# Attention beside a small expert: the output matrix M built by head groups, its rows placed by DMA, and two spread products on GpSimd

## The chip, the cores and the metric

One NeuronCore of one Trainium2 chip. The metric is device time in microseconds of one execution; lower is better. Engines are called PE (TensorE), DVE (VectorE), ACT (ScalarE), POOL (GpSimd) and SP (SyncE, which only issues DMAs here). PSUM has eight banks of 512 float32 columns, numbered 0 to 7.

## The reference

x has 2048 rows (tokens) of D = 640 columns in bfloat16. It is normalized, and three terms are added:

```python
xn = _layernorm(x)                                  # per row
# A: linear attention, H = 32 heads of Dh = 20 columns
qkv = (xn @ wqkv); q, k, v = ...                    # each 2048 x 640
phi = lambda t: jnp.where(t > 0, t + 1, jnp.exp(t)) + 1e-6
pq, pk = phi(q), phi(k)
kv = einsum("bhsd,bhse->bhde", pk, v)               # 20 x 20 for each head
z  = einsum("bhsd->bhd", pk)
o  = (pq @ kv) / (pq . z + 1e-6)                    # for each head and token
A  = o @ wo
# B: the 8 tokens with the largest xn @ w_r go through a gated MLP of F = 1536
y  = (silu(x_sel @ w_gate) * (x_sel @ w_up)) @ w_down * sigmoid(r_sel)
B  = xn + scatter of y to the 8 rows
out = x + A + B
```

## The kernel before

The order of the work on each engine is the order in which the program is written: nothing is scheduled by a planner. Tokens come in T = 16 tiles of 128.

First stage (to about 57 us in the profile): each tile is normalized, transposed into `xnT`, multiplied by the k weights (L249), turned into `pk` by exp and relu on ACT and a minimum and add on DVE (`k_phi`, L271), and summed into G = xn^T pk (`g1`, L278). Blocks of q, 128 columns by 512 tokens, are put in between: `q_mm(u)` (L286) on PE, `q_act` (L295, L296) on ACT, and `q_phi` (L302) on DVE, which writes `pqT`. Blocks 0 to 7 are made here, 8 to 19 later; block u belongs to tokens (u // 5) x 512 and rows (u % 5) x 128 of `pqT`. `eq` and `rq` have three buffers each. POOL makes x + xn in place of x (`add_s`, L219); SP stores it to `s_dram` (L110), because the expert's rows are added there by a scatter, and later loads it back into `x_sb` (L769).

Denominators: `den(h)` (L584) makes 1 / (pq . z) for half h of the tokens, as rows by heads. They have to be spread from 32 heads to 640 rows of `pqT`. For half 0 this goes through DRAM: ACT stores `rden` repeated 20 times to `rd` (L623), SP loads it as `spr`, in two DMAs (`rden_in`, L629), and DVE multiplies `pqT` by it for 256 tokens at a time (`rden_mul(j)`, L636, j = 0 to 3; tokens j x 256, that is output tiles 2j and 2j + 1). For half 1 it goes through PE (`spread_mm`, L596), ACT (`spread_copy`, L610) and DVE (`spread_mul`, L617), between output tiles.

The middle stage: kv = G^T wv for six heads at a time (`kv_mm`, L642; 120 columns, the sixth group 40), masked to the head blocks by `kv_out` (L650) and written to `kvz`. Then M = blockdiag(kv) wo, 640 x 640, which needs 128-row blocks for the output product. A group has 120 rows, so `kvz` is laid out with zeros between the groups (offset 248), and `m_unit(m)` makes the 128 rows of block m from the two groups that touch it: two groups by two halves of 320 columns, four products (L661) and one copy to `Ms` (L666). `kvz` is zeroed by a memset on DVE at the start (L136). The expert runs here too: gate and up products (L720), the down product (L749), and its four column pieces times the gate, taken from one PSUM bank by ACT and DVE in turn (L761, L763) into `y8`; POOL scatters `y8` onto `s_dram` (L764). The order on PE from there is q12, the down product, q13, unit 0, q14, unit 1, q15, unit 2, q16, unit 3, q17, unit 4, q18, q19, with q blocks in banks 2 and 3 in turn.

The output stage: for each tile t, `o_mm(t)` (L799) multiplies `pqT` by `Ms` in ten products of 320 columns, `o_out(t)` (L808) adds `x_sb` on DVE and starts the store, on SP for even t and ACT for odd t (L813). Banks alternate, so tile t + 2 waits for `o_out(t)`. After tile 0 PE does `den(1)`, which reads the q blocks 10 to 19. The last tile (`o_last`) goes out in three pieces: 320 and 160 columns by SP, and 160 by ACT (L837).

DMAs issued from SP and ACT use eight semaphores in turn; a DMA waits until the one that used its semaphore before has landed. DMAs of one issuing engine are issued in program order.

Of the kernel before, what the change touches and what calls it, by code (L numbers as in the profile page):

```python
# [8 lines left out]
P = 128  # L9
S = 2048  # L10
D = 640
# [3 lines left out]
T = S // P  # L15
KC = D // P
FC = F // P
C = 8
HW = 320
HG = 120  # L20
NG = 6
WS = 248
KVW = 1664
FJ = F // 4
QW = D // 4
EPS_BF16 = 1.0013580322265625e-05
# [2 lines left out]
BF16 = mybir.dt.bfloat16  # L29
# [4 lines left out]
ALU = mybir.AluOpType  # L34
# [3 lines left out]
def kernel(  # L38
# [12 lines left out]
    nc = tc.nc  # L51
    V, A, G, PE = nc.vector, nc.scalar, nc.gpsimd, nc.tensor
# [15 lines left out]
    ps = psum.tile([P, 8, 512], F32, tag="ps", name="ps")  # L68
    rd = tc.dram_tile([4, D, 256], BF16, name="rd")
# [9 lines left out]
    wv = big.tile([P, KC, D], BF16, tag="wv", name="wv")  # L79
    wo = big.tile([P, NG, D], BF16, tag="wo", name="wo")  # L80
    wg = big.tile([P, KC, F], BF16, tag="wg", name="wg")
    wu = big.tile([P, KC, F], BF16, tag="wu", name="wu")
    wd = big.tile([P, FC, D], BF16, tag="wd", name="wd")
    kvz = big.tile([P, KVW], BF16, tag="kvz", name="kvz")

    SP = nc.sync
# [32 lines left out]
    def load_cols(w, lo, hi, base):  # L119
        SP.dma_start(w[:, lo:hi, :], wqkv_v[:, lo:hi, base : base + D])  # L120

    w_jobs = {
        6: [lambda: kcw(wg, B_w_gate, 0, 3)], 8: [lambda: kcw(wg, B_w_gate, 3, 5)],
        10: [lambda: kcw(wu, B_w_up, 0, 3)], 12: [lambda: kcw(wu, B_w_up, 3, 5)],
        13: [lambda: load_cols(wv, 0, 3, 2 * D), lambda: load_cols(wv, 3, 5, 2 * D), load_wo],
    }

    def load_wd(lo, hi):
        SP.dma_start(wd[:, lo:hi, :], B_w_down.rearrange("(fc p) n -> p fc n", p=P)[:, lo:hi, :])

    w_jobs[14] = [lambda: load_wd(0, 6), lambda: load_wd(6, FC)]

    zw = sb("zw", [P, 512])
    V.memset(zw[:], 0.0)
    xsT = sb("xsT", [P, KC, H])
    V.memset(kvz[:], 0.0)  # L136
    V.memset(xsT[:], 0.0)
    mhalf = sb("mhalf", [P, 2])
    G.memset(mhalf[:], -0.5)
# [143 lines left out]
    def q_mm(u, bank=7):  # L283
        tb, m = u // KC, u % KC
        for kc in range(KC):
            PE.matmul(  # L286
                ps[:, bank, :], lhsT=wq[:, kc, m * P : (m + 1) * P],
                rhs=xnT[:, kc, tb * 512 : (tb + 1) * 512],
                start=(kc == 0), stop=(kc == KC - 1),
            )  # L290

    def q_act(u, bank=7):
        e = evq.tile([P, 512], BF16, tag="eq", name=f"eq{u}")
        r = evq.tile([P, 512], BF16, tag="rq", name=f"rq{u}")
        A.activation(e[:], ps[:, bank, :], AF.Exp)  # L295
        A.activation(r[:], ps[:, bank, :], AF.Relu)  # L296
        kev["q", u] = e, r

    def q_phi(u):
        tb, m = u // KC, u % KC  # L300
        e, r = kev.pop(("q", u))
        V.scalar_tensor_tensor(  # L302
            out=pqT[:, m, tb * 512 : (tb + 1) * 512], in0=e[:], scalar=1.0, in1=r[:],
            op0=ALU.min, op1=ALU.add,
        )

    def q_ev(u, bank=7):
        q_act(u, bank)
        q_phi(u)
# [315 lines left out]
            rden[:, 0, :].unsqueeze(1).to_broadcast([P, DH, 256]),  # L625
        )

    def rden_in(j):
        SP.dma_start(  # L629
            spr[:, j * KC : (j + 2) * KC, :],  # L630
            rd[j : j + 2, :, :].rearrange("j (m p) t -> p (j m) t", p=P),
        )

    def rden_mul(j):
        sl = pqT[:, :, j * 256 : (j + 1) * 256]
        V.tensor_tensor(out=sl, in0=sl, in1=spr[:, j * KC : (j + 1) * KC, :], op=ALU.mult)  # L636

    def kv_mm(gs, bank):
        for i, g in enumerate(gs):
# [6 lines left out]
                )  # L646

    def kv_out(g0, n, w, bank, o):
        a = P + WS * g0
        V.tensor_tensor(  # L650
            out=kvz[0:w, a : a + WS * n].rearrange("p (g f) -> p g f", g=n)[:, :, 0:w],
            in0=ps[0:w, bank, o : o + n * w].rearrange("p (g f) -> p g f", g=n),
            in1=mask[0:w, 0:w].unsqueeze(1).to_broadcast([w, n, w]), op=ALU.mult,
        )

    def m_unit(m, b0, eng):
        for i, g in enumerate((m, m + 1)):
            w = HG if g < 5 else 40
            a = g * 256 + (P if i == 0 else 0)
            for b in range(2):  # L660
                PE.matmul(  # L661
                    ps[:, b0 + b, 0:HW], lhsT=kvz[0:w, a : a + P],
                    rhs=wo[0:w, g, b * HW : (b + 1) * HW], start=(i == 0), stop=(i == 1),
                )
        dst = Ms[:, m, :].rearrange("p (b f) -> p b f", b=2)
        eng(dst, ps[:, b0 : b0 + 2, 0:HW])  # L666


    for t in range(T):
# [37 lines left out]
    spare = big.tile([P, T, D], BF16, tag="xn", name="spare")  # L707
    spr = spare[:, 0:8, :].rearrange("p a b -> p (a b)").rearrange("p (r f) -> p r f", f=256)
    Ms = late[:, 0:KC, :]
    for j in (0, 2):  # L710
        rden_in(j)
    A.copy(GT[:, 0:4, 512:D], ps[:, 2, :].rearrange("p (c f) -> p c f", c=4))
    A.copy(GT[:, 4, 512:D], ps[:, 3, 0:P])
    kv_mm(range(0, 4), 4)
# [2 lines left out]
    for a, w in enumerate((wg, wu)):  # L717
        for kc in range(KC):
            for j in range(4):
                PE.matmul(  # L720
                    ps[32 * j : 32 * j + 32, a, 0:FJ].rearrange("p (b f) -> p b f", f=32), lhsT=xsT[:, kc, :],
                    rhs=w[:, kc, :].rearrange("p (b j f) -> p j b f", j=4, f=32)[:, j],
                    start=(kc == 0), stop=(kc == KC - 1), tile_position=(0, 32 * j),
                )
    eg = late[:, 9:13, :].bitcast(F32).rearrange("p a b -> p (a b)")[:, 0 : 2 * FJ]
    eg = eg.rearrange("p (a b) -> p a b", a=2)
    ub = late[:, 5, 0:FJ]
# [14 lines left out]
    V.tensor_mul(hm, gu, eg[:, 1, :])  # L742
    hT = late[:, 8, 0:FJ]
    V.transpose(hT, hm)
    q_ev(11, 2)
    q_mm(12, 3)
    for fc in range(FC):
        for i in range(4):
            PE.matmul(  # L749
                ps[32 * i : 32 * i + 32, 1, 0:QW], lhsT=hT[:, 32 * fc : 32 * fc + 32],  # L750
                rhs=wd[:, fc, i * QW : (i + 1) * QW],
                start=(fc == 0), stop=(fc == FC - 1), tile_position=(0, 32 * i),
            )
    q_ev(12, 3)
    q_mm(13, 2)
    y8 = sb("y8", [C, D])
    for i in range(4):
        y_o, y_i = y8[:, i * QW : (i + 1) * QW], ps[32 * i : 32 * i + C, 1, 0:QW]
        g_i = gate[32 * i : 32 * i + C, 2:3]
        if i % 2:  # L760
            V.tensor_scalar(out=y_o, in0=y_i, scalar1=g_i, scalar2=None, op0=ALU.mult)  # L761
        else:
            A.activation(y_o, y_i, AF.Identity, scale=g_i)  # L763
# [1 line left out]
        s_dram[:, :], bass.IndirectOffsetOnAxis(ap=idx_i[0:C, 0:1], axis=0), y8[:], None,  # L765
        compute_op=ALU.add,
    )
    for a in range(0, T, 4):
        nc.sync.dma_start(  # L769
            x_sb[:, a : a + 4, :],  # L770
            s_dram[a * P : (a + 4) * P, :].rearrange("(t p) d -> p t d", p=P),
        )
    m_unit(0, 4, V.tensor_copy)
    q_ev(13, 2)
    q_mm(14, 3)
    q_ev(14, 3)
    m_unit(1, 6, A.copy)
    q_mm(15, 2)
    q_ev(15, 2)
    rden_mul(0)  # L780
    m_unit(2, 4, V.tensor_copy)
    q_mm(16, 3)
    q_ev(16, 3)
    m_unit(3, 6, A.copy)
    rden_mul(1)
    q_mm(17, 2)
    m_unit(4, 0, V.tensor_copy)
    q_ev(17, 2)
    q_mm(18, 3)
    q_ev(18, 3)  # L790
    q_mm(19, 2)
    q_ev(19, 2)
    rden_mul(2)

    def o_mm(t):
        b0 = 2 * (t % 2)
# [18 lines left out]
    def o_last(t):  # L815
        o_t = evk.tile([P, 2, HW], BF16, tag=("ek", "rk")[t % 2], name=f"o{t}")
        of = o_t[:].rearrange("p b f -> p (b f)")
        for i, (lo, w) in enumerate(((0, HW), (HW, QW), (HW + QW, QW))):
            if i == 2:
                PE.matmul(  # L820
                    ps[:, 4 + i, 0:w], lhsT=ident[:], rhs=x_sb[:, t, lo : lo + w],
                    start=True, stop=False,
                )
            for kc in range(KC):
                PE.matmul(  # L825
                    ps[:, 4 + i, 0:w], lhsT=pqT[:, kc, t * P : (t + 1) * P],
                    rhs=Ms[:, kc, lo : lo + w], start=(kc == 0 and i < 2), stop=(kc == KC - 1),
                )
            if i < 2:
                V.tensor_tensor(  # L830
                    out=of[:, lo : lo + w], in0=ps[:, 4 + i, 0:w], in1=x_sb[:, t, lo : lo + w],
                    op=ALU.add,
                )
            else:
                A.copy(of[:, lo : lo + w], ps[:, 4 + i, 0:w])  # L835
            eng = nc.scalar if i == 2 else nc.sync
            eng.dma_start(out_v[:, t, lo : lo + w], of[:, lo : lo + w])  # L837

    H1 = ([0, 1], [2, 3], [4])
    for t in range(T - 1):  # L840
        o_mm(t)
        if t == 0:
            den(1, 4)
        if t in (1, 3, 5):
            spread_mm(1, H1[t // 2], 4)
            for i in range(2):
                spread_copy(1, H1[t // 2], 4, i)
        o_out(t)
        if t == 0:
            rden_mul(3)  # L850
        if t in (2, 4, 6):
            for i in range(2):
                spread_mul(1, H1[t // 2 - 1], 4, i)
# [29 lines left out]
```

## Time and profile before

| | |
|---|---|
| median of 3 runs | 115.75 us (114.96 to 115.82) |
| the profiled execution | 115.16 us, of which the span of the profile is 113.4 us |
| PE busy | 107.3 us (95%) |
| DVE, ACT, POOL busy | 82.6, 64.7, 48.3 us (73%, 57%, 43%) |
| granted TensorE clock | 1.00 |
| the four costliest groups on PE | L249 25.1, L286 24.8, L799 21.4, L278 19.6 us |

A row of the timeline has the start in us, the duration in us (of a merged group, from its first start to its last end), the engine, the line, the operation, what it writes and reads, and the count; in brackets, the idle time before it and what ended that. A row of a grouped view has the line, engine, operation, operands, shape and count, then the busy time in us and the mean of one in ns, then the idle time of the engine before it. A DMA row has the KB of each and the time from issue to landing in us. A row of the chain has start, duration and what. An engine name with q behind it is its queue.

### The profile page before, as it was taken

To read this page: it belongs to the slowest core of one execution; us is meant where nothing else is said; L and a number is where in the kernel's file an instruction comes from. 1 tells how busy PE (TensorE), PEld (TensorE's weight loads), DVE (VectorE), ACT (ScalarE), POOL (GpSimd) and SP (SyncE) were. 2 spreads that over 40 slices of the span, in tenths; PEclk is the share of its full clock that TensorE was granted. 3 is DMA by queue.
4 is the path that set the end of the run, shared out by engine and by line. 5 is a ranking of instruction groups with operands and counts; after the bars stand their busy time and mean duration, and the time that the engine had idled before them with its cause. 6 is when DMAs were issued, how large, how long until landed. Compare 5 with 4: busy or idle time off the path is not lost.

```text
span 113.4 us, 2472 instructions
## 1 busy us (share of the span) xinstructions
PE 107.3 (95%) x891; PEld 63.0 (56%) x891; DVE 82.6 (73%) x174; ACT 64.7 (57%) x165; POOL 48.3 (43%) x92
## 2 busy tenths in 40 slices
PE   5999999999999999999999999999999999999950
PEld 2346644546555555565447797465546666767740
DVE  3889798999988977544749523868697798865550
ACT  1469988678686776755058354769876656000010
POOL 6604478451878589999997230005000000000000
PEclk9999999999999999999999999999999999999999
DMA  3999948304989999799999999549189933333341
GB/s 101 328 264 331 383 129 85 65 6 88 300 245 284 71 277 299 188 388 221 197 352 380 386 386 343 163 121 310 40 234 374 364 134 116 116 118 116 115 151 32
DMA packets 27360, 24.39 MB, mean 215 GB/s; under 512 B 8555, under 2 KB 26067, under 8 KB 27347
## 3 DMA queue, kind: packets, MB, share of 16 engines
q1 hardware_dynamic: 21817, 17.29, 55.5%
q10 hardware_dynamic: 5498, 6.92, 18.5%
q8 instruction: 7, 0.11, 0.4%
q14 instruction: 6, 0.05, 0.2%
q0 software_dynamic: 32, 0.01, 0.1%
HBM read 15.73 MB, written 6.56 MB: 197 GB/s over the span
## 4 chain that ended last, share of the span: by engine, by line
PE 80%; POOL 6%; DVE 5%; ACT 4%; issue 1%; POOLq 0%
PE ps L799 18%; PE ps L286 16%; PE ps L278 14%; PE ps L249 13%; PE ps L519 4%; PE ps L147 4%; POOL rs L188 3%; PE ps L661 2%; DVE stats L176 2%; PE ps L720 2%; PE ps L642 2%; PE ps L584 1%; POOL t L187 1%; PE ps L825 1%; DVE xn L197 1%
## 5 line engine op out<-in xcount | busy, mean ns | idle before, releaser
L249 PE MATMUL ps<-wk,xnT 128*128 128x320 bf16 (+1 forms) x160 | 25.1, 300 | 0.3 <-ACT xnT L233 0.2
L286 PE MATMUL ps<-xnT,wq 128*128 128x512 bf16 x100 | 24.8, 379 | 0.3
L799 PE MATMUL ps<-late,pqT 128*128 128x320 bf16 x150 | 21.4, 299 | 0.0
L249 PEld LDWEIGHTS <-xnT 128*128 128x128 bf16 x160 | 15.2, 98 | 8.5 <-ACT xnT L233 0.8
L278 PE MATMUL ps<-pk,xn 128*128 128x512 bf16 x80 | 19.6, 379 | 0.0
L295 ACT ACTIVATE eq<-ps 128x512 bf16<-128x512 f32 x20 | 11.9, 597 | 13.2 <-PE ps L286 13.1
L302 DVE SCALAR_TENSOR_TENSOR pqT<-eq,rq 128x512 bf16<-128x512 bf16 x20 | 14.6, 731 | 6.5 <-ACT rq L296 6.5
L271 DVE SCALAR_TENSOR_TENSOR pk<-ek,rk 128x640 bf16<-128x640 bf16 x16 | 14.1, 893 | 5.9 <-ACT rk L264 5.7
L219 POOL TENSOR_SCALAR x_sb<-x_sb,rs,nm 128x640 bf16<-128x640 bf16 x16 | 17.6, 1107 | 0.8
L799 PEld LDWEIGHTS <-pqT 128*128 128x128 bf16 x150 | 14.3, 98 | 6.4 <-issue 0.6
L263 ACT ACTIVATE ek<-ps 128x320 bf16<-128x320 f32 x32 | 14.4, 451 | 4.5 <-PE ps L249 4.5
L808 DVE TENSOR_TENSOR o<-ps,x_sb 128x640 bf16<-128x640 f32 x15 | 12.3, 823 | 5.2 <-PE ps L799 4.6
L286 PEld LDWEIGHTS <-wq 128*128 128x128 bf16 x100 | 9.2, 97 | 11.5 <-issue 1.2
L176 DVE BATCH_NORM_STATS2 stats<-x_sb 128x6 f32<-128x320 bf16 x32 | 14.4, 480 | 0.9 <-DMA x_sb<-in_A_x_dram 0.9
L264 ACT ACTIVATE rk<-ps 128x320 bf16<-128x320 f32 x32 | 14.6, 455 | 0.0
L278 PEld LDWEIGHTS <-xn 128*128 128x128 bf16 x80 | 7.6, 98 | 7.6
L296 ACT ACTIVATE rq<-ps 128x512 bf16<-128x512 f32 x20 | 11.8, 592 | 0.0
L187 POOL TENSOR_SCALAR t<-mv 128x1 bf16<-128x1 f32 x9 | 3.9, 428 | 13.2 <-DVE mv L178 13.1
L835 ACT CAST o<-ps 128x160 bf16<-128x160 f32 x1 | 0.3, 293 | 12.9 <-PE ps L825 12.9
L188 POOL TENSOR_TENSOR rs<-t,mhalf 128x1 f32<-128x1 bf16 x9 | 6.8, 761 | 0.7
L610 ACT CAST spare<-ps 128x1024 bf16<-128x1024 f32 (+1 forms) x6 | 4.9, 872 | 3.2 <-PE ps L596 3.2
L197 DVE TENSOR_SCALAR xn<-x_sb,mv,rs 128x640 bf16<-128x640 bf16 x11 | 4.8, 434 | 1.3 <-POOL rs L188 0.7
(125 smaller groups left out, 113.7 us busy)
## 6 DMA issues: line engine op xcount, KB each, us to landing
s_dram<-x_sb SPq DMA_DIRECT2D x4, 640.0 KB, 9.9
x_sb<-s_dram SPq DMA_DIRECT2D x4, 640.0 KB, 5.7
wd<-in_B_w_down_dram SPq DMA_DIRECT2D x2, 960.0 KB, 9.8
x_sb<-in_A_x_dram SPq DMA_DIRECT2D x2, 640.0 KB, 8.6
rd<-rden ACTq DMA_DIRECT2D x1, 1280.0 KB, 8.1
spare<-rd SPq DMA_DIRECT2D x2, 640.0 KB, 7.0
out_dram<-o SPq DMA_DIRECT2D x8, 160.0 KB, 1.8
wg<-in_B_w_gate_dram ACTq DMA_DIRECT2D x1, 1152.0 KB
```

The costliest lines, as they stand in the source:

```text
L176: V.bn_stats(out=stats[:, t, b, :], in_=x_sb[:, t, b * HW : (b + 1) * HW])
L219: G.tensor_scalar(out=x_sb[:, t, :], in0=x_sb[:, t, :], scalar1=rs1[:, sl], scalar2=nm[:, sl], op0=ALU.mult, op1=ALU.add,)
L249: PE.matmul(ps[:, b0 + b, 0:n], lhsT=xnT[:, kc, t * P : (t + 1) * P], rhs=wk[:, kc, b * HW : b * HW + n], start=(kc == 0), stop=(kc == KC ...
L263: A.activation(e[:, b, :], ps[:, b0 + b, 0:HW], AF.Exp)
L264: A.activation(r[:, b, :], ps[:, b0 + b, 0:HW], AF.Relu)
L271: V.scalar_tensor_tensor(out=pk[:, t, :].rearrange("p (b f) -> p b f", b=2), in0=e[:], scalar=1.0, in1=r[:], op0=ALU.min, op1=ALU.add,)
L278: PE.matmul(ps[:, 2 + c, :], lhsT=xn[:, t, c * P : (c + 1) * P], rhs=pk[:, t, 0:512], start=(t == 0), stop=(t == T - 1),)
L286: PE.matmul(ps[:, bank, :], lhsT=wq[:, kc, m * P : (m + 1) * P], rhs=xnT[:, kc, tb * 512 : (tb + 1) * 512], start=(kc == 0), stop=(kc == K ...
L295: A.activation(e[:], ps[:, bank, :], AF.Exp)
L302: V.scalar_tensor_tensor(out=pqT[:, m, tb * 512 : (tb + 1) * 512], in0=e[:], scalar=1.0, in1=r[:], op0=ALU.min, op1=ALU.add,)
L799: PE.matmul(ps[:, b0 + b, 0:HW], lhsT=pqT[:, kc, t * P : (t + 1) * P], rhs=Ms[:, kc, b * HW : (b + 1) * HW], start=(kc == 0), stop=(kc == ...
L808: V.tensor_tensor(out=o_t[:], in0=ps[:, b0 : b0 + 2, 0:HW], in1=x_sb[:, t, :].rearrange("p (b f) -> p b f", b=2), op=ALU.add,)
```

## The change

M is made by groups: unit g has two products (its 120 rows of kv, or 40, times wo), six units in all. Group 0's rows are copied to `Ms` directly; the others are copied to `Mst` at their own partitions, and SP moves them to the partitions of the 128-row blocks, in two DMAs for groups 1 to 4 and one for group 5. `kvz` has no gaps and no memset. `rden_mul(1)` and `rden_mul(3)` go to POOL, behind the scatter; `rden_mul(0)` and `(2)` stay on DVE. The loads of `wv`, `wd` and the spread denominators are one DMA each instead of two. q15 to q19 follow one another in five banks (0, 2, 3, 6, 7), behind all M units. The down product's four pieces lie in two banks. The reload of `x_sb` is issued behind the row DMAs. The last tile's second and third pieces leave in one DMA from ACT, so SP issues only the first.

```diff
-        13: [lambda: load_cols(wv, 0, 3, 2 * D), lambda: load_cols(wv, 3, 5, 2 * D), load_wo],
+        13: [lambda: load_cols(wv, 0, KC, 2 * D), load_wo],
...
-    w_jobs[14] = [lambda: load_wd(0, 6), lambda: load_wd(6, FC)]
+    w_jobs[14] = [lambda: load_wd(0, FC)]
...
-    V.memset(kvz[:], 0.0)
...
-    def rden_in(j):
+    def rden_in():
         SP.dma_start(
-            spr[:, j * KC : (j + 2) * KC, :],
-            rd[j : j + 2, :, :].rearrange("j (m p) t -> p (j m) t", p=P),
-        )
-
-    def rden_mul(j):
+            spr[:, 0 : 4 * KC, :], rd[:, :, :].rearrange("j (m p) t -> p (j m) t", p=P)
+        )
+
+    def rden_mul(j, eng):
         sl = pqT[:, :, j * 256 : (j + 1) * 256]
-        V.tensor_tensor(out=sl, in0=sl, in1=spr[:, j * KC : (j + 1) * KC, :], op=ALU.mult)
+        eng.tensor_tensor(out=sl, in0=sl, in1=spr[:, j * KC : (j + 1) * KC, :], op=ALU.mult)
...
+    def m_unit(g, b0, eng):
+        w = HG if g < 5 else 40
+        for b in range(2):
+            PE.matmul(
+                ps[0:w, b0 + b, 0:HW], lhsT=kvz[0:w, g * HG : g * HG + w],
+                rhs=wo[0:w, g, b * HW : (b + 1) * HW], start=True, stop=True,
+            )
+        dst = (Ms if g == 0 else Mst)[0:w, g, :].rearrange("p (b f) -> p b f", b=2)
+        eng(dst, ps[0:w, b0 : b0 + 2, 0:HW])
+        up = min(8 * g, w) if g < 5 else w
+        if g:
+            o = P - 8 * g
+            SP.dma_start(Ms[o : o + up, g - 1, :], Mst[0:up, g, :])
+        if 0 < g < 5:
+            SP.dma_start(Ms[0 : w - up, g, :], Mst[up:w, g, :])
...
     V.transpose(hT, hm)
+    m_unit(0, 6, V.tensor_copy)
     q_ev(11, 2)
     q_mm(12, 3)
+    m_unit(1, 4, A.copy)
+    q_act(12, 3)
     for fc in range(FC):
         for i in range(4):
             PE.matmul(
-                ps[32 * i : 32 * i + 32, 1, 0:QW], lhsT=hT[:, 32 * fc : 32 * fc + 32],
+                ps[32 * i : 32 * i + 32, i % 2, 0:QW], lhsT=hT[:, 32 * fc : 32 * fc + 32],
...
-    q_ev(12, 3)
-    q_mm(13, 2)
...
+    m_unit(2, 6, V.tensor_copy)
+    q_phi(12)
+    q_mm(13, 2)
+    m_unit(3, 4, V.tensor_copy)
+    q_ev(13, 2)
+    m_unit(4, 6, A.copy)
+    q_mm(14, 3)
+    m_unit(5, 4, V.tensor_copy)
+    q_ev(14, 3)
+
+    def reload(a):
+        SP.dma_start(
             x_sb[:, a : a + 4, :],
             s_dram[a * P : (a + 4) * P, :].rearrange("(t p) d -> p t d", p=P),
         )
...
+    for a in range(0, T, 4):
+        reload(a)
+    rden_mul(1, G)
+    rden_mul(3, G)
+    q_mm(15, 0)
+    q_ev(15, 0)
+    rden_mul(0, V)
+    for u, b in ((16, 2), (17, 3), (18, 6), (19, 7)):
+        q_mm(u, b)
+        q_ev(u, b)
...
-            eng = nc.scalar if i == 2 else nc.sync
-            eng.dma_start(out_v[:, t, lo : lo + w], of[:, lo : lo + w])
+            if i == 0:
+                nc.sync.dma_start(out_v[:, t, 0:HW], of[:, 0:HW])
+        nc.scalar.dma_start(out_v[:, t, HW:], of[:, HW:])
...
-            rden_mul(3)
+            rden_mul(2, V)
```

More of the change, by code (lines that the diff above doesn't have):

```diff
@@ L21 @@
 NG = 6
-WS = 248
-KVW = 1664
+KVW = D
 FJ = F // 4
@@ L648, in kv_out @@
     def kv_out(g0, n, w, bank, o):
-        a = P + WS * g0
+        a = HG * g0
         V.tensor_tensor(
-            out=kvz[0:w, a : a + WS * n].rearrange("p (g f) -> p g f", g=n)[:, :, 0:w],
+            out=kvz[0:w, a : a + w * n].rearrange("p (g f) -> p g f", g=n),
             in0=ps[0:w, bank, o : o + n * w].rearrange("p (g f) -> p g f", g=n),
@@ L654, in kv_out @@
         )
[L656 to L663, printed above, removed]
-                )
-        dst = Ms[:, m, :].rearrange("p (b f) -> p b f", b=2)
-        eng(dst, ps[:, b0 : b0 + 2, 0:HW])
+    def m_unit(g, b0, eng):
[13 more added lines that the diff above has]
+            SP.dma_start(Ms[0 : w - up, g, :], Mst[up:w, g, :])
     for t in range(T):
@@ L709 @@
     Ms = late[:, 0:KC, :]
-    for j in (0, 2):
-        rden_in(j)
+    rden_in()
     A.copy(GT[:, 0:4, 512:D], ps[:, 2, :].rearrange("p (c f) -> p c f", c=4))
@@ L724 @@
                 )
+    Mst = big.tile([P, NG, D], BF16, tag="wg", name="Mst")
     eg = late[:, 9:13, :].bitcast(F32).rearrange("p a b -> p (a b)")[:, 0 : 2 * FJ]
@@ L749 @@
             PE.matmul(
-                ps[32 * i : 32 * i + 32, 1, 0:QW], lhsT=hT[:, 32 * fc : 32 * fc + 32],
+                ps[32 * i : 32 * i + 32, i % 2, 0:QW], lhsT=hT[:, 32 * fc : 32 * fc + 32],
                 rhs=wd[:, fc, i * QW : (i + 1) * QW],
                 start=(fc == 0), stop=(fc == FC - 1), tile_position=(0, 32 * i),
+                skip_group_check=True,
             )
-    q_ev(12, 3)
-    q_mm(13, 2)
     y8 = sb("y8", [C, D])
     for i in range(4):
-        y_o, y_i = y8[:, i * QW : (i + 1) * QW], ps[32 * i : 32 * i + C, 1, 0:QW]
+        y_o, y_i = y8[:, i * QW : (i + 1) * QW], ps[32 * i : 32 * i + C, i % 2, 0:QW]
         g_i = gate[32 * i : 32 * i + C, 2:3]
@@ L767 @@
     )
-    for a in range(0, T, 4):
-        nc.sync.dma_start(
+    m_unit(2, 6, V.tensor_copy)
[9 more added lines that the diff above has]
+        SP.dma_start(
             x_sb[:, a : a + 4, :],
@@ L772 @@
         )
[L773 to L793, printed above, removed]
+    for a in range(0, T, 4):
[8 more added lines that the diff above has]
+        q_ev(u, b)
     def o_mm(t):
```

## The prediction

> **What bounds the kernel now.** I read the page first: busy time of each engine, then the chain that ended last; after that the same chain in order of time, the timelines by engine around the changed lines, and the DMA issues.
>
> ```profile
> span 113.4 us, 2472 instructions
> PE 107.3 (95%) x891; PEld 63.0 (56%) x891; DVE 82.6 (73%) x174; ACT 64.7 (57%) x165; POOL 48.3 (43%) x92
> PE 80%; POOL 6%; DVE 5%; ACT 4%; issue 1%; POOLq 0%
> ```
>
> TensorE is busy for 95% of the span and carries 80% of the chain. The part that the change touches, in order of time:
>
> ```profile
> 67.98 1.10 PE ps L642 x20
> ...
> 71.45 2.27 PE ps L286 x10
> 73.72 0.94 PE ps L749 x48
> 74.67 1.18 PE ps L286 x5
> 75.85 0.55 PE ps L661 x4
> ...
> 82.36 0.65 PE ps L661 x4
> 83.01 2.26 PE ps L286 x10
> 85.27 1.36 PE ps L799 x10
> 86.63 0.83 PE ps L584 x20
> 87.46 1.47 PE ps L799 x10
> ...
> 107.95 1.02 PE ps L825 x10
> ```
>
> Between 71.45 and 108.97 us the chain never leaves TensorE: q blocks (L286), the expert's down product (L749), the M units (L661), then output tiles (L799). Whatever shortens this stretch counts in full, and whatever makes TensorE wait counts in full. One place has little slack: den (L584) needs the last q block, and reads it as soon as VectorE has made it.
>
> ```profile
> 86.42 0.69 DVE L302 SCALAR_TENSOR_TENSOR pqT<-eq,rq 128x512 bf16<-128x512 bf16 x1 [0.39 <-ACT rq L296]
> L636 DVE TENSOR_TENSOR pqT<-pqT,spare 128x1280 bf16<-128x1280 bf16 x4 | 3.3, 817 | 0.0
> ```
>
> That last q_phi ends at 87.11; den ends and the second output tile starts at 87.46, 0.35 later. So the end of the last q_phi sets the start of the output phase. The forecast turns on it.
>
> **M by groups.** A unit was four products of 320 columns, 0.55 us (the last one 0.65): 4 x 0.55 + 0.65 = 2.85 for five. Six units of two products are 12 x 0.1375 = 1.65. Gain 1.2 us on the path. Units 4 and 5 reuse banks whose copies sit on VectorE behind y8 and q_phi(12); I find them some 0.1 us late each. Net gain 1.0.
>
> **The nine row DMAs.** Units 1 to 5 go to Mst and then by SP to Ms. On SP they stand behind the load of the spread denominators and ahead of the four reloads of x.
>
> ```profile
> L629 SPq DMA_DIRECT2D spare<-rd x2: 360/504/649, 73.8 to 74.2; - x2
> 81.41 2.38 SPq L769 DMA_DIRECT2D x_sb<-s_dram  x4
> spare<-rd SPq DMA_DIRECT2D x2, 640.0 KB, 7.0
> x_sb<-s_dram SPq DMA_DIRECT2D x4, 640.0 KB, 5.7
> DMA to landing us min/median/max: 1.5/1.8/4.2
> grep<-grep SPq DMA_DIRECT2D x3, 40.0 KB, 9.8
> ```
>
> The fifth row is the view of the output tensor's DMAs, up to 160 KB each. The spread load goes out in two DMAs, the second starting at 74.2, and is whole at 74.2 + 7.0 = 81.2; one DMA of both moves the same bytes. In the order of waits, the second DMA of unit 4 reuses that load's semaphore, so it goes out only then, and unit 5's DMA 0.5 later. Its landing is bounded by 1.5 us (the fastest output row) and 9.8 (grep, 40 KB behind other loads). The load ahead has landed by then, so I take the output rows' median, 1.8: Ms is whole at 81.2 + 0.5 + 1.8 = 83.5. Without other waits the first output tile would start at 84.1 and read the rows of units 4 and 5 at 84.65: hidden by 1.1 us, and wholly where the wait described next decides. Behind them the reloads go out at 82.2 instead of 81.41; the first add comes only after the last q_phi, which hides that 0.8.
>
> **Two spread products on GpSimd.** VectorE loses two of the 0.82 us products of L636. POOL's rows show no such product, but they show what happens when POOL and VectorE both read SBUF:
>
> ```profile
> 30.00 0.88 POOL L208 TENSOR_SCALAR xn<-x_sb,rs,nm 128x640 bf16<-128x640 bf16 x1
> 30.25 1.30 DVE L271 SCALAR_TENSOR_TENSOR pk<-ek,rk 128x640 bf16<-128x640 bf16 x1
> 17.73 1.57 DVE L271 SCALAR_TENSOR_TENSOR pk<-ek,rk 128x640 bf16<-128x640 bf16 x2
> 60.81 0.91 POOL L219 TENSOR_SCALAR x_sb<-x_sb,rs,nm 128x640 bf16<-128x640 bf16 x1
> 61.07 1.18 DVE L302 SCALAR_TENSOR_TENSOR pqT<-eq,rq 128x512 bf16<-128x512 bf16 x1
> 57.91 0.88 POOL L219 TENSOR_SCALAR x_sb<-x_sb,rs,nm 128x640 bf16<-128x640 bf16 x1
> 58.32 0.28 DVE L558 TENSOR_TENSOR allc<-ps,iota_f 128x128 f32<-128x128 f32 x1
> ```
>
> L271 takes about 0.8 (two in 1.57) and 1.30 when it meets a long POOL instruction: it ends at 31.55, so its own 0.8 began at 30.74, just before POOL's end at 30.88. So does q_phi: 0.69 alone, 1.18 beside POOL. The VectorE add with one operand in PSUM ran at 0.28 in the middle of a POOL instruction. So VectorE's operations with two SBUF inputs (q_phi and L636) take turns with POOL, one whole instruction at a time, and o_out, which reads PSUM, does not. Who goes first when both queue:
>
> ```profile
> 17.98 0.67 POOL L187 TENSOR_SCALAR t<-mv 128x1 bf16<-128x1 f32 x1
> 49.65 0.23 POOL L471 TENSOR_SCALAR rs<-rs 128x2 f32<-128x2 f32 x1
> ```
>
> A POOL operation of 0.23 us alone took 0.67: it asked at 17.98, waited for the first of the two L271 at 17.73 and was done at 18.65, before the second ended at 19.30, though that second one stood ready. Turns alternate.
>
> The price of one product: 0.23 for two elements and 0.88 for 640 give 1.02 ns an element, so 1280 elements are 1.53 us if one operand sets the pace (lower bound), 0.23 + 2 x 1280 x 1.02 = 2.84 if the two operands are fetched in turn, and 4 x 0.88 = 3.5 as an upper bound (four 640-element passes). I take 2.84, because both operands lie in SBUF and the only POOL rows of length read one; VectorE can go on 0.14 earlier (30.74 against 30.88), so it is kept out for 2.70. The Trainium skill, "GPSIMD Engine Reference", section 3.1, gives about 2.6 cycles an element at 1.2 GHz for a product of two inputs; by that the instruction would be an estimated 2.8 us and the sum below the same; no run here shows it yet.
>
> Now the queue for SBUF from the landing at 81.2. VectorE is in q_phi(15) then: TensorE ends q15 at 71.45 + 5 x 1.1 (q blocks) + 1.65 (M) + 0.94 (L749) + 0.2 (waits) = 79.75, and q_phi follows 1.15 later, as the last one did (85.27 to 86.42), at 80.9. GpSimd's first product asks, gets its turn, and rden_mul(0), which stands next on VectorE, waits; then the second product asks and q_phi(16) waits. All of it goes before the last q_phi ends: 80.9 + 5 x 0.69 + 0.82 + 2 x 2.70 = 90.6. Before it was 87.11, so the output phase starts 3.5 us later, at 90.95 instead of 87.46. This swallows the 1.0 gained on M. The first output tile waits too, for rden_mul(0), but den's wait ends last. Behind the waiting q_phis on VectorE stand o_out(0) and rden_mul(2); TensorE asks for neither before its third output tile, at 92.4. Both products are over by 88, so the output tiles that need them, 2 and 6, find them done, and from there the output phase is as before.
>
> **q in five banks** lets TensorE run its last five q blocks without waiting for ScalarE. It ends them by 79.75 + 4 x 1.1 = 84.15 and then waits for the same q_phi: nothing gained while den waits. If it didn't, it is part of the 1.0 above. The y8 halves in two banks save waits between VectorE and ScalarE, but ScalarE reaches them after unit 1's copy and q_act(12), so the scatter starts about when it did; what waits for it, the reloads, is hidden.
>
> **The tail.**
>
> ```profile
> 109.34 1.23 SPq L837 DMA_DIRECT2D out_dram<-o  x2
> 109.75 0.34 ACTq L837 DMA_DIRECT2D out_dram<-o  x1
> out_dram<-o ACTq DMA_DIRECT2D x1, 40.0 KB, 1.5
> out_dram<-o SPq DMA_DIRECT2D x1, 40.0 KB, 1.9
> ```
>
> SP's second piece goes out at 109.34 + 1.23 - 0.33 = 110.24 and lands at 112.15; ScalarE's, issued at 109.75, is already in at 111.25. In one DMA of 80 KB on ScalarE's queue the landing takes between 1.5 and 1.9 (the output's median above is 1.8): I take 1.75, so 111.5. Gain 0.65, between 0.5 and 0.9.
>
> **Costed at nothing.** The kvz memset and the joined loads:
>
> ```profile
> L136 DVE MEMSET kvz<- 128x832 uint32 x1 | 0.8, 752 | 0.1
> L176 DVE BATCH_NORM_STATS2 stats<-x_sb 128x6 f32<-128x320 bf16 x32 | 14.4, 480 | 0.9 <-DMA x_sb<-in_A_x_dram 0.9
> 44.67 1.11 SPq L120 DMA_DIRECT2D wv<-in_A_wqkv_dram  x2
> 51.11 0.99 SPq L129 DMA_DIRECT2D wd<-in_B_w_down_dram  x2
> ```
>
> After the memset VectorE waits 0.9 us for x's first tile, so its 0.75 is free. wv and wd are issued 23 us ahead of their first use (L642 at 67.98, L749 at 73.72); even at 9.8 us to land they are early.
>
> **Sum.** +3.5 at the output phase's start and -0.65 at the tail: span 113.4 + 2.85 = 116.25. The profiled execution took 115.16, 1.76 around its span: 118.0. It lies 0.6 under the median of the runs (115.75), so I leave the sum as it is. With 1.53 and 3.5 for the GpSimd product (1.39 and 3.36 held), the last q_phi ends at 88.0 or 91.9 and the time is 115.4 or 119.3. This case's own range is 115.4 to 119.4.
>
> **Rivals.**
> *GpSimd's products don't hold VectorE up*, because a product of two inputs lets it in between, or is short. For: no row shows VectorE against a long two-input POOL operation. Against: every single-input one did hold it. Then the gains stand: 115.16 - 1.0 - 0.65 = 113.5.
> *VectorE keeps its turn while it has work*, and GpSimd gets gaps only. Then q_phi(15), rden_mul(0), q_phi(16) and (17) run to 83.8, the first product takes the gap before q_phi(18) to 86.5, and the last q_phi ends at 87.9. The second product holds rden_mul(2) to 90.6, and o_out(1) behind it ends at 92.2, so TensorE's fourth output tile, due at about 90.7 before (87.46, two tiles and the spread between them), starts 1.5 late: 115.16 + 1.5 - 0.65 = 116.0. Against it stands the POOL operation at 17.98.
> *Ms is late*, with no wait for GpSimd: the last row DMA takes the longest time of an output row, 4.2 instead of 1.8, because the scatter and other rows are ahead of it. Ms is then whole at 85.9 instead of 83.5 and the first output tile waits 1.25 for it: 113.5 + 1.25 = 114.75. From 2.95 us on (84.65 less 81.7) this decides; the queue that is empty by then speaks against it.
> *TensorE's clock falls while it waits*. In the forecast it does almost nothing from 86.5 to 90.6.
>
> ```profile
> 1.24 4.02 PE L147 MATMUL ps<-zw 128*128 128x512 bf16 x9 [1.24 <-DVE zw L134]
> ```
>
> At the start nine products of 512 columns took 4.02 us, 0.45 each; the ten of q11 and q12 took 2.27, 0.23 each. The same stretch again would add 2.0: 120.0. The Trainium skill, "TensorE: Matmul & The Clock Gate", Part 1, has the half clock return after an idle window of about 3.4 us; den's short pieces break up this idle time, and nothing before shows such a gap.
>
> **How the numbers follow.** Forecast 0.55, clock 0.10, VectorE keeps its turn 0.10, Ms late 0.08, no hold-up 0.17. Predicted time 118.0. The range 113.6 to 120.2 leaves out about half of the lowest and the highest case. A change of 1% (1.15 us) is about what a measurement of this kernel tells from none. Slower: 0.51 of the forecast, the clock, 0.04 of the third: 0.65. Faster: the last case and 0.02 of late Ms: 0.19. Same: the rest, 0.16.
>
> **What would show it.** POOL rows of the two products near 2.8 us from 81.2 on; rden_mul(0) and q_phi(16) with spans of 3 us and more instead of 0.82 and 0.69; the last q_phi ending near 90.6 and den spread over several us; M products in twelve of 0.14; the last DMA landing 0.65 earlier after the last product. Wrong if q_phi stays at 0.69 beside POOL, if the products are short, or if the first output tile waits for a DMA of Mst.

## The result, and the profile after

The changed kernel takes 118.72 us (117.93 to 119.57) against 115.51 in the runs of the kernel before beside it: a ratio of 1.0285, 95% interval 1.0201 to 1.0369, so it is slower. The profiled execution took 117.93, with a span of 116.2. In the other three the granted clock was 0.985, 0.971 and 0.985, and the span 117.0, 117.8 and 117.0.

Each ratio below leaves out a kernel's runs that lie over 1.5% above its fastest: none of the kernel before, but 2 of 4 with all products on VectorE, 4 of 12 without the joined tail and 8 of 12 with the reloads on GpSimd's queue, whose medians over all runs (116.12, 115.31 and 116.07) are not clearly below the 115.28, 115.32 and 115.61 of the kernel before.

The page after: span, busy time, the chain by engine, and the groups of the GpSimd products (L633) and of q_phi (L300).

```profile
span 116.2 us, 2463 instructions
...
PE 105.9 (91%) x874; PEld 62.6 (54%) x883; DVE 85.2 (73%) x172; ACT 64.8 (56%) x165; POOL 54.6 (47%) x94
...
PE 39%; DMA 15%; POOL 11%; DVE 11%; ACT 9%; issue 8%; POOLq 3%; SPq 2%; DVEq 0%
...
L633 POOL TENSOR_TENSOR pqT<-pqT,spare 128x1280 bf16<-128x1280 bf16 x2 | 5.9, 2996 | 2.4 <-DMA spare<-rd 2.4
...
L300 DVE SCALAR_TENSOR_TENSOR pqT<-eq,rq 128x512 bf16<-128x512 bf16 x20 | 16.7, 841 | 5.1 <-ACT rq L294 5.0
```

By the page TensorE is busy 1.4 us less in a span 2.8 us longer, so it idles 4.2 us more; a little of that isn't real, since 874 matmuls are recorded for 883 weight loads. Its part of the chain falls from 80% to 39%. About 10 us of that, a twelfth of the span, is the stretch from 81.3 to 91.2 below; the rest lies before 70.24, where the chain now runs back through GpSimd's gather of the expert's tokens and the load of wd. The chain in order of time (start, length, what) has left TensorE in the middle:

```profile
70.24 1.81 PE ps L721 x40
...
77.94 0.71 PE ps L657 x4
78.65 1.08 PE ps L284 x5
80.10 1.20 PE ps L284 x5
81.82 0.60 ACT rq L294
82.44 0.69 DVE pqT L300
83.14 3.15 DVE pqT L633
86.28 4.21 DVE pqT L300 x3
90.50 0.70 DVE pqT L300
91.53 1.47 PE ps L803 x10
```

From 82.44 to 91.19 it runs through VectorE. The timelines of GpSimd, VectorE and TensorE (start, busy time, engine, line, operation, count, and in brackets the idle time before and who ended it):

```profile
82.80 5.95 POOL L633 TENSOR_TENSOR pqT<-pqT,spare 128x1280 bf16<-128x1280 bf16 x2 [2.43 <-DMA spare<-rd]
...
82.44 0.69 DVE L300 SCALAR_TENSOR_TENSOR pqT<-eq,rq 128x512 bf16<-128x512 bf16 x1 [0.81 <-ACT rq L294]
83.05 3.23 DVE L633 TENSOR_TENSOR pqT<-pqT,spare 128x1280 bf16<-128x1280 bf16 x1
86.20 4.99 DVE L300 SCALAR_TENSOR_TENSOR pqT<-eq,rq 128x512 bf16<-128x512 bf16 x4
...
86.34 1.53 PE L803 MATMUL ps<-late,pqT 128*128 128x320 bf16 x10 [0.73 <-DVE pqT L633]
...
89.34 0.29 PE L582 MATMUL ps<-pqT,zm 128*32 128x256 bf16 x4 [1.15 <-DVE pqT L300]
...
91.25 0.28 PE L582 MATMUL ps<-pqT,zm 128*32 128x256 bf16 x2 [0.41 <-DVE pqT L300]
```

rden_mul(0) spans 3.23 us instead of 0.82. Of the four q_phis, 4.99 us together, three run at 0.69, so the first took about 3.1. den (L582) is strung out behind them, and the second output tile starts at 91.53 instead of 87.46. That is +4.07; the output tiles take back 0.15 and the tail 1.1, which leaves the +2.8 of the spans.

### The profile page after: what moved, and what is told of

Same layout as the page of the kernel before. It is cut to its first block, busy times and chain, and to the rows that moved or that the text cites. A ratio compares the mean times of both kernels' runs of the same rounds, so it can differ in the third digit from the quotient of the medians.

```text
span 116.2 us, 2463 instructions
## 1 busy us (share of the span) xinstructions
PE 105.9 (91%) x874; PEld 62.6 (54%) x883; DVE 85.2 (73%) x172; ACT 64.8 (56%) x165; POOL 54.6 (47%) x94
## 4 chain that ended last, share of the span: by engine, by line
PE 39%; DMA 15%; POOL 11%; DVE 11%; ACT 9%; issue 8%; POOLq 3%; SPq 2%; DVEq 0%
PE ps L803 17%; DMA wd<-in_B_w_down_dram 12%; PE ps L284 8%; DVE pqT L300 5%; PE ps L247 4%; DMA x_sb<-in_A_x_dram 4%; PE ps L276 3%; DVE pqT L633 3%; ACT ek L261 3%; POOLq L570 2%; ACT rk L262 2%; ACT rq L294 2%; PE ps L657 2%; PE ps L721 2%; SPq L344 2%
## 5 line engine op out<-in xcount | busy, mean ns | idle before, releaser
L284 PE MATMUL ps<-xnT,wq 128*128 128x512 bf16 x94 | 23.6, 379 | 0.7 <-issue 0.3
L300 DVE SCALAR_TENSOR_TENSOR pqT<-eq,rq 128x512 bf16<-128x512 bf16 x20 | 16.7, 841 | 5.1 <-ACT rq L294 5.0
L217 POOL TENSOR_SCALAR x_sb<-x_sb,rs,nm 128x640 bf16<-128x640 bf16 x16 | 18.1, 1139 | 0.8
L269 DVE SCALAR_TENSOR_TENSOR pk<-ek,rk 128x640 bf16<-128x640 bf16 x16 | 13.6, 863 | 5.5 <-ACT rk L262 5.4
L633 POOL TENSOR_TENSOR pqT<-pqT,spare 128x1280 bf16<-128x1280 bf16 x2 | 5.9, 2996 | 2.4 <-DMA spare<-rd 2.4
```

What stands on the lines that cost most here:

```text
L217: G.tensor_scalar(out=x_sb[:, t, :], in0=x_sb[:, t, :], scalar1=rs1[:, sl], scalar2=nm[:, sl], op0=ALU.mult, op1=ALU.add,)
L269: V.scalar_tensor_tensor(out=pk[:, t, :].rearrange("p (b f) -> p b f", b=2), in0=e[:], scalar=1.0, in1=r[:], op0=ALU.min, op1=ALU.add,)
L284: PE.matmul(ps[:, bank, :], lhsT=wq[:, kc, m * P : (m + 1) * P], rhs=xnT[:, kc, tb * 512 : (tb + 1) * 512], start=(kc == 0), stop=(kc == K ...
L300: V.scalar_tensor_tensor(out=pqT[:, m, tb * 512 : (tb + 1) * 512], in0=e[:], scalar=1.0, in1=r[:], op0=ALU.min, op1=ALU.add,)
```

## The experiments

**All four products on VectorE**, the rest of the change kept:

```diff
-    rden_mul(1, G)
-    rden_mul(3, G)
...
+        if u in (17, 19):
+            rden_mul((u - 15) // 2, V)
...
-            rden_mul(2, V)
+            rden_mul(3, V)
```

> The changed kernel with all four spread products back on VectorE (0 behind q15, 1 behind q17, 2 behind q19, 3 behind the first output add); all else stays. Theory (VectorE's two-operand work and GpSimd's products take turns for SBUF, one whole instruction at a time, and this alone makes the change slower): no q_phi longer than 0.75 us in this stretch, the last q_phi ends about 1.2 us behind q19 (near 86.7 instead of 91.2), time 118.7 - 4.0 = 114.7 or a little less, faster than before (115.5). Rival (the row DMAs or the new order of q make it slower, and GpSimd only fills the time): the first output tile still waits, time at or above 117.5.

Ratio to before 0.9911 [0.9848, 0.9975]; the profiled execution took 114.04 us. The timeline of VectorE:

```profile
85.80 1.51 DVE L300 SCALAR_TENSOR_TENSOR pqT<-eq,rq 128x512 bf16<-128x512 bf16 x2
```

No q_phi is held any more, the last ends at 87.30, and the second output tile starts at 87.64. The whole loss comes with the two products on GpSimd; without them the change gains about 1 us (by the interval, 0.3 to 1.8).

**The two products alone, on the kernel before** (GpSimd's stand behind unit 1 of M):

```diff
     m_unit(1, 6, A.copy)
+    rden_mul(1, G)
+    rden_mul(3, G)
...
-    rden_mul(1)
...
-    rden_mul(2)
...
-            rden_mul(3)
+            rden_mul(2)
```

> The kernel before with spread products 1 and 3 on GpSimd, behind the scatter, and nothing else changed. Theory: the first product takes its turn at 81.7 behind rden_mul(0), q16's q_phi waits to 84.5, the second product takes the next turn and q17's q_phi waits to 87.9; the last q_phi ends near 89.9 instead of 87.1 and the time is 115.5 + 2.8 = 118.3. Rival (GpSimd is harmless here): 115.5 or less, since VectorE has 1.6 us less to do.

1.0266 [1.0205, 1.0327], 118.48 us. VectorE's timeline has two held instructions again, a q_phi and rden_mul(0):

```profile
81.25 2.39 DVE L302 SCALAR_TENSOR_TENSOR pqT<-eq,rq 128x512 bf16<-128x512 bf16 x1 [0.94 <-ACT rq L296]
83.57 3.23 DVE L636 TENSOR_TENSOR pqT<-pqT,spare 128x1280 bf16<-128x1280 bf16 x1
```

So the collision doesn't need the new M: ahead of the last q_phi it makes this kernel 3.1 us slower too. In the profile the last q_phi ends 3.55 later than before (90.66 against 87.11); 0.93 of that is a later start of gate/up (69.94), not the collision.

**The joined last DMA alone, on the kernel before.**

```diff
-            eng = nc.scalar if i == 2 else nc.sync
-            eng.dma_start(out_v[:, t, lo : lo + w], of[:, lo : lo + w])
+            if i == 0:
+                nc.sync.dma_start(out_v[:, t, 0:HW], of[:, 0:HW])
+        nc.scalar.dma_start(out_v[:, t, HW:], of[:, HW:])
```

> The kernel before with only the last tile's second and third pieces in one DMA of ScalarE's queue. By the prediction's term the end comes 0.65 us earlier: 114.85. By the changed kernel's trace, where the span ended 2.6 us after the last copy instead of 3.7, it is 1.1: 114.4. Rival (what was gained at the tail of the changed kernel came from its other DMAs' semaphores): 115.5, no change.

114.82 us, 0.9952 [0.9899, 1.0004]: the interval reaches from a gain of 1.2 us to none, so the times alone decide neither between the two sizes nor against the rival. From the end of ScalarE's last copy to the end of the span, its profile has 3.34 us against 3.72 before, a gain of 0.4.

**Each GpSimd product in five parts of 256 columns.**

```diff
-    rden_mul(1, G)
-    rden_mul(3, G)
+    for j in (1, 3):
+        for m in range(KC):
+            sl = pqT[:, m, j * 256 : (j + 1) * 256]
+            G.tensor_tensor(out=sl, in0=sl, in1=spr[:, j * KC + m, :], op=ALU.mult)
```

> The changed kernel with each GpSimd product cut into five of 256 columns, one for each 128 rows of pqT. By the row of GpSimd's product (2.8 us for 1280) a part is about 0.75 us and keeps VectorE out for 0.6. Theory (turns alternate instruction by instruction): from q15's q_phi on VectorE has five more operations, one part goes before each: the last q_phi ends at 83.1 + 0.8 + 4 x 0.69 + 5 x 0.6 = 89.7 instead of 91.2 and the time is 117.2. Rival one (GpSimd keeps SBUF while its queue has work): all ten parts go first, the last q_phi ends near 94 and the time is about 121. Rival two (VectorE goes first when both wait): the last q_phi ends near 87, about 114.8.

115.37 us, 0.9981 [0.9938, 1.0025]: 1.8 less than the theory expected. The timelines:

```profile
82.86 9.25 POOL L793 TENSOR_TENSOR pqT<-pqT,spare 128x256 bf16<-128x256 bf16 x10 [2.90 <-DMA spare<-rd]
...
83.48 4.39 DVE L300 SCALAR_TENSOR_TENSOR pqT<-eq,rq 128x512 bf16<-128x512 bf16 x4
```

The four q_phis take 1.15 us each: one short part goes in front of each, and costs it 0.47. So the turns alternate as expected, but the price was too high: 0.47, not 0.6, and four parts, not five, since rden_mul(0) started at 82.74, before the first part. The last q_phi ends at 87.87, not 89.7. What a turn costs follows the length of GpSimd's instruction (0.47 here, 2.41 for the whole product); only the parts whose turn falls ahead of the last q_phi cost anything.

**One product on GpSimd, started after the last q_phi**, the other three on VectorE. GpSimd first copies four columns that the last q_phi wrote, and so has to wait for it.

```diff
-    rden_mul(1, G)
-    rden_mul(3, G)
...
+        if u in (17, 19):
+            rden_mul((u - 15) // 2, V)
+    late_pq = pqT[:, KC - 1, 2044:2048]
+    G.tensor_copy(xsT[:, KC - 1, 0:4], late_pq)
+    rden_mul(3, G)
...
-            rden_mul(2, V)
+            pass
```

> The changed kernel with products 0, 1 and 2 on VectorE and only product 3 on GpSimd, started after the last q_phi (a copy of four columns that the last q_phi wrote stands ahead of it on GpSimd). Theory (the loss is the collision with the last q_phis, not GpSimd's slowness): GpSimd runs it from about 87.5 to 90.3 us, VectorE's next two-operand work from SBUF comes at about 89 (product 2) and 92, so only product 2 may be held for 1 to 2 us, which no output tile notices; q_phi as without GpSimd, last one ends at 87.3, the time is that of the kernel with all four on VectorE, 114.0 to 114.9. Rival (a long GpSimd product costs whatever runs beside it, output tiles too): 116 or more.

114.45 us, 0.9921 [0.9887, 0.9956], like all four on VectorE. The timelines of GpSimd and VectorE:

```profile
89.16 2.60 POOL L633 TENSOR_TENSOR pqT<-pqT,spare 128x1280 bf16<-128x1280 bf16 x1
...
89.06 0.82 DVE L815 TENSOR_TENSOR o<-ps,x_sb 128x640 bf16<-128x640 f32 x1
90.32 0.82 DVE L815 TENSOR_TENSOR o<-ps,x_sb 128x640 bf16<-128x640 f32 x1 [0.45 <-PE ps L806]
```

The output adds, which read PSUM, run at 0.82 beside it. Here, where VectorE has no operation with two SBUF inputs beside it, the product costs nothing that shows, but it gains nothing either: VectorE is not the bound.

**M by groups without the joined tail** (and without GpSimd): the three last DMAs as before.

> The changed kernel with all four products on VectorE and the last three pieces sent by three DMAs as before: of the change only M by groups, the joined loads and the q banks are left. Theory (M nets -1.0 us, the tail has its price apart): 114.5 to 114.9, that is 0.5 to 0.8 below before and 0.3 to 1.1 above the kernel with the joined tail; from the last copy on ScalarE to the end of the span 3.3 to 3.7 us instead of 2.55. Rival (the tail gains only some 0.5, as it did on the kernel before, and the M stretch the rest): 114.5 or less, and M would have gained over 1.0. Rival 2 (M gains nothing by the clock): 115.3.

0.9939 [0.9898, 0.9979], some 0.7 us less than before by the ratio, within what the theory expected; the median of all twelve runs, 115.31, is that of the kernel before (115.32). The tail missed: 2.90 us from the last copy to the end of the span instead of 3.3 to 3.7.

**One-input multiplications on GpSimd** by a constant, in place of the products.

```diff
+        if eng is G:
+            eng.tensor_scalar(out=sl, in0=sl, scalar1=0.5, scalar2=None, op0=ALU.mult)
+            return
```

> The changed kernel with the two GpSimd products as one-input multiplications by a constant, in place (it leaves out the spread denominators of half of the first 1024 tokens). Theory (whole instructions take turns, and GpSimd's price goes with its SBUF operands): 1.4 to 1.9 us each instead of 2.8 and 3.2, the two held VectorE instructions about as long; last q_phi ends near 88.3, the output phase starts 2.5 us sooner than in the changed kernel, 115.8 to 116.4. Rival 1 (price goes by the elements alone): 2.8 us each again, 118.7. Rival 2 (a one-input GpSimd operation does not hold VectorE): q_phi stays at 0.69, time 114.3.

Ratio 1.0386 [1.0304, 1.0468]; all three expectations missed. The timelines:

```profile
82.67 7.39 POOL L634 TENSOR_SCALAR pqT<-pqT 128x1280 bf16<-128x1280 bf16 x2
...
82.28 7.88 DVE L300 SCALAR_TENSOR_TENSOR pqT<-eq,rq 128x512 bf16<-128x512 bf16 x1
```

A multiplication with one operand fewer lasted longer, not less long, and VectorE got no turn between the two. Two further kernels ask why.

**Two-operand form without the wait for the load**: the slice times itself.

> The changed kernel with each GpSimd product as a tensor_tensor of the slice with itself (it leaves out the spread denominators of half of the first 1024 tokens), so that it waits for no load, as the one-input products did, but has the two-operand form. Theory (the form decides who gets the next turn): 2.6 to 3.2 us each, one VectorE instruction gets its turn between the two, none lasts longer than 3.5 us. Rival (two products that both stand ready keep VectorE out until both are done, whatever their form): one VectorE instruction of 5.5 us or more.

**The one-input form in five parts each.**

> The changed kernel with each one-input multiplication by a constant in five parts of 256 columns (it leaves out the spread denominators of half of the first 1024 tokens). Theory (the one-input form on GpSimd lets VectorE in only when nothing more of it is ready): parts of 0.8 us, ten in a row, one VectorE instruction of 7 to 8 us, about 121 us. Rival (VectorE gets a turn after each instruction, and the two long ones were a chance of their timing): q_phi of 1.2 to 1.6 us each, 115 to 117.

The squares took 118.47 us in their one run, the parts 118.89. GpSimd and VectorE, first the squares, then the parts:

```profile
79.92 5.10 POOL L634 TENSOR_TENSOR pqT<-pqT 128x1280 bf16<-128x1280 bf16 x2
...
79.56 6.03 DVE L300 SCALAR_TENSOR_TENSOR pqT<-eq,rq 128x512 bf16<-128x512 bf16 x1
```

```profile
84.52 10.38 POOL L793 TENSOR_SCALAR pqT<-pqT 128x256 bf16<-128x256 bf16 x10
...
88.60 2.51 DVE L300 SCALAR_TENSOR_TENSOR pqT<-eq,rq 128x512 bf16<-128x512 bf16 x3
```

With the squares the rival holds: one q_phi of 6.03 us, behind both products. With the parts, the q_phis last 0.69 to 0.92 us, and VectorE is hardly held. So taking turns is what the products of this change did, not a rule; two GpSimd instructions that both stand ready can keep VectorE out through both. What decides isn't settled. Both products go ahead of the last q_phi either way, and the time is alike, 118.47 against 118.72; but in both runs TensorE's clock fell as well, so these times don't price the hold-up alone (the last section shows where).

**The loads of wv and wd split again**, all products on VectorE:

```diff
-    w_jobs[14] = [lambda: load_wd(0, FC)]
+    w_jobs[14] = [lambda: load_wd(0, 6), lambda: load_wd(6, FC)]
```

(and wv in the same way).

> The kernel with all four products on VectorE, and wv and wd loaded by two DMAs each as before. Theory (the joined loads cost nothing; the slow register loads of the token gather vary from run to run): within 0.4 us of the joined ones, 114.0 to 114.8, gate/up products start anywhere from 69.0 to 70.2. Rival (the joined loads slow the gather down): gate/up starts at 69.0, and the time is 0.8 to 1.1 lower, 113.2.

114.52 us, 0.9914 [0.9878, 0.995]: in time the theory holds. The start of gate/up, 69.36, fits both. TensorE's timeline at the gate/up products and later:

```profile
69.36 0.99 PE L721 MATMUL ps<-wg,xsT 128*32 128x384 bf16 x20 [0.28 <-POOL xsT L571]
...
85.51 0.99 PE L803 MATMUL ps<-late,pqT 128*128 128x320 bf16 x6 [0.24 <-DMA late<-Mst]
...
89.62 2.99 PE L803 MATMUL ps<-late,pqT 128*128 128x320 bf16 x20 [0.67 <-DVE o L812]
```

Gate/up start 0.73 sooner than in the kernel with joined loads and all products on VectorE (70.09), but the lead is lost again: TensorE waits for the last row move, then for the first output add, which waits for the reload of x (issued at 84.11 and landed 4.5 later; the add starts at 88.75).

**The reloads issued from GpSimd's queue**, so that they don't stand behind the row moves on SP (`SP.dma_start` becomes `G.dma_start`), with joined and with split loads.

> All four products on VectorE, joined loads, and the four reloads of the residual issued from GpSimd's queue instead of SP's, where they stand behind the nine row moves. Theory (the row moves hold the reload's issue back: 83.45 in the kernel with all products on VectorE against a scatter that landed at 82.09; before it was 81.41 against 81.39): issue within 0.5 us of the scatter's landing, first reload lands about 1 us sooner, which takes off the 0.2 us that the first output add waited: 0.0 to 0.4 us less than 114.4. Rival (a transfer issued by GpSimd takes longer to land): landing no sooner, the same time or up to 1 us more.

> The same with wv and wd loaded by two DMAs each. Theory (with the split loads TensorE came 0.73 us sooner to the output tiles, and lost 0.24 us to the last row move and 0.67 us to the first output add, which waited for the reload): the 0.67 goes, 113.6 to 114.1, against 114.5 with the reloads on SP. Rival (the lead is lost elsewhere, or the reload lands no sooner from GpSimd's queue): 114.4 or more.

Joined: 0.9927 [0.9884, 0.997]. Split: the six runs spread from 113.38 to 120.11 (median 117.18), so no ratio is given. The reload does go out 0.3 us after the scatter lands in both, but the first one takes 5.4 and 4.8 us to land instead of 4.7 and 4.5, and TensorE with split loads still waits 0.33 for the first add. No gain is shown. By their ratios (0.991 to 0.994) the kernels without a GpSimd product ahead of the last q_phi beat both kernels, and none of them is clearly beyond another. Two of them, the late product and the split loads, also have a median over all twelve runs (114.45 and 114.52) below that of the kernel before, 115.32.

## Why the prediction was right, point by point

**The hold-up by GpSimd was the right mechanism**, shown by taking it away, by doing it alone, by shortening it and by moving it. Its terms were off, in opposite directions. A product lasts 2.60 alone (predicted 2.84), a little below the estimate of 2.8 from the Trainium skill, "GPSIMD Engine Reference", section 3.1. VectorE was held for 2.41 (3.23 - 0.82) and about 2.4, not 2.70 each: 0.6 too much in the sum. q_phi(15) started at 82.44 instead of 80.9: 1.5 too little. The spans of neighbouring VectorE instructions overlap a little, which the sum left out: 0.35. So the last q_phi ended at 91.19 instead of 90.6.

**Why q_phi(15) was late: a step that failed.** The prediction let TensorE reach the middle stage when it did before. But the gate/up products wait for the gather of the expert's eight tokens on GpSimd, and that ended later. GpSimd's register loads of the indices, in the view of their line, before and then after (shortest, median and longest ns, first and last start):

```profile
L572 POOLq TENSOR_LOAD <-idx_i x8: 299/495/636, 61.2 to 67.5; - x8
```

```profile
L570 POOLq TENSOR_LOAD <-idx_i x8: 290/648/976, 60.8 to 68.6; - x8
```

and in the timeline after the product that waits for the last copy:

```profile
70.24 1.00 PE L721 MATMUL ps<-wg,xsT 128*32 128x384 bf16 x20 [1.04 <-POOL xsT L571]
```

Gate/up began at 70.24, not 69.01, so the gain on M was spent before M began. What delayed the gather isn't shown. The joined loads are suspect: they were costed at nothing, because wd is in long before its use, and over all profiles the gate/up start is 69.84 to 72.20 with joined loads (nine kernels) and 69.01 to 69.94 with split ones (five). But there is one profile of each, the ranges touch, and the kernel before with two products on GpSimd has split loads, register loads nearly as long (302, 616 and 966 ns), a wait of 1.27 us, and in its chain

```profile
69.94 1.81 PE ps L720 x40
```

The times don't decide it either, since the split version was no faster.

**The spread load was late as well**, a second step that failed. The prediction had it whole at 81.2. It went out at 73.89, and the row move that reuses its semaphore (as the prediction said) was released only at 82.67. In the view of SP's waits (total, times, longest):

```profile
SPq L668 <- DMA spare<-rd: 0.9, 1, 0.9
```

That is 8.8 us for the one DMA, where the two took 7.0 each, and GpSimd's first product began at 82.80, not 81.2. rden_mul(0) needs this load too, so had q15 been on time, VectorE would still have stood at rden_mul(0) until about 82.7. The late gather and the late load, some 1.5 us each, fell side by side and counted once. The likely cause is the joining, which the prediction passed over with "one DMA of both moves the same bytes": the kernel with split wv and wd, which keeps the one spread DMA, has 9.0 us (73.34 to 82.32), and the kernel before with two products on GpSimd, which keeps the two, has 6.9. No run changes this load alone.

**M by groups**: from the end of kv to the end of the last q block 12.92 us after (72.69 to 85.61) against 13.82: 0.9 with the waits for banks, 1.0 predicted. **Row moves**: wholly hidden in the changed kernel, since no output tile waits for Mst. But the last went out at 83.60, not 81.7, because of the load, so the 1.1 us of cover that the prediction gave them weren't there: where TensorE came sooner, in the two kernels with split loads and all products on VectorE, the first output tile waited 0.24 and 0.41 for them. **q in five banks**: nothing, as predicted.

**The tail**: 0.65 predicted, 1.1 measured (2.58 us from the last copy to the end of the span, 3.72 before). By landing, the step was about right: before, the last piece was in 2.43 us after the last copy (112.15 against 109.72); with only the joined DMA added it is 1.64 (110.53 + 1.6 against 110.49), 0.8 sooner. But the span ends later than the landing, which the prediction left out, and there joining gives only 0.3 to 0.4: 3.72 to 3.34 on the kernel before, 2.90 to 2.57 on the changed one without GpSimd's products. The other 0.8 came with the rest of the change (3.72 to 2.90 with the three last DMAs as before). It fits that the row moves shift the semaphores round: in the kernel with only the joined DMA, SP waits for the last transfer first (1.7 us in one wait) and has the other semaphores still to pass; in the changed kernel it waits 1.4 in three places. That this order is the whole 0.8 isn't shown.

**The sum** was 116.25 for the span; 116.2 was measured. The agreement is partly luck: 4.07 instead of 3.5 at the output phase, 1.1 instead of 0.65 at the tail. Of the rivals, none took place in the profiled run. "No hold-up" would have been 113.5; the kernels without one took about 114.4. In their profiles M's gain is gone again: with joined loads gate/up start 1.1 later, with split ones 0.35 later, and the output phase then waits 0.9 for the row move and the reload. The clock stayed at full speed through den's gaps in the profiled run. In the other three it was 0.971 to 0.985, and no trace shows where it fell; it may be part of the 0.7 between prediction and median, and it may be the clock rival in part, since that rival did occur in the kernel of the squares (last section).

## What to carry to other kernels

In these runs a product moved to GpSimd was free only where VectorE had no operation with two SBUF inputs beside it; ahead of the last link of a chain it cost nearly its own length (2.41 of 2.60 us), whatever VectorE's share of busy time said. Before moving it, ask which VectorE instruction is the next to be waited for, and start the GpSimd work behind that one. When a change joins or moves loads, compare everything else that runs beside them, small reads and other DMAs too: here the gather and the spread load each came 1.2 to 1.5 us later than assumed, and neither stood in the sum.

## What was not expected of the hardware

Two ready GpSimd instructions overlap in the record: the second of the squares began 0.54 us before the first ended (5.10 for two of 2.82), and VectorE stayed out for 6.03. The Trainium skill, "SBUF — State Buffer", section "SBUF: two separate sides", has whoever starts first hold the shared port pair for its whole instruction. The change's products agree; the one-input parts don't, as q_phis of 0.69 to 0.92 ran while GpSimd was busy throughout.

TensorE's clock fell after waits, but not after all of them. In the profile of M by groups without the joined tail it waited 2.34 us for the gather and then ran the gate/up products at about half speed:

```profile
PEclk9999999999999999999999999599999999999999
```

That is the page's row of the granted clock, in 40 slices; the timeline at the dip:

```profile
71.25 1.50 PE L721 MATMUL ps<-wg,xsT 128*32 128x384 bf16 x20 [2.34 <-POOL xsT L571]
72.52 1.82 PE L721 MATMUL ps<-wu,xsT 128*32 128x384 bf16 x20
```

The same products take 0.99 at full clock. The kernel of the one-input parts waited 3.30 and had 1.79 and 1.82; but the one with the late product waited 2.50 and kept 0.99. It happened at the output phase too. In the kernel of the squares TensorE stood for 2.68 us ahead of the first output tile, which then took 2.29 instead of 1.53; the page's row of the clock, and the chain:

```profile
PEclk9999999999999999999999999999997699999999
88.31 2.29 PE ps L804 x10
```

The kernel before with two products on GpSimd stood for 2.71 at the same place and kept 1.52. So a wait of some 2.3 to 3.3 us may or may not cost about another 1.5 us, and what decides isn't known. In the changed kernel den's rows break the idle time into gaps of at most 1.15 us.
